# Attention with a local window, then a gated feed-forward: value products in 64-row tiles over two banks, merged ahead of the next scores in two of six units, and another plan

## The chip, the cores and the metric

The kernel runs on one core of a Trainium2 chip. The time of a kernel is the device time of one execution in microseconds; it is given as the median of the runs shown, with the lowest and highest. A profile is one further execution, recorded by the hardware profiler; it has a time of its own.

## The reference, cut to what matters

Each query sees the first 8 keys and the last 96 (its own included). A bias falls with the distance, with a slope for each head. The attention's output goes through two projections whose product is projected back.

```python
scores = scale * np.matmul(q, k.transpose(0, 1, 3, 2))
dist = np.where(is_global & ~is_local, float(n_local), np.abs(rel).astype(np.float32))
scores = np.where(keep, scores + bias, -1e9)          # bias = -slope[head] * dist
a = np.exp(scores - np.max(scores, axis=-1, keepdims=True))
a = a / (np.sum(a, axis=-1, keepdims=True) + 1e-09)
attn = np.matmul(a, v)                                # 4 x 8 heads x 768 x 64
x = attn.transpose(0, 2, 1, 3).reshape(B * S, H * D)  # 3072 x 512
out = (x @ w_a) * (x @ w_b) @ w_out                   # d_ff 1536
```

All inputs are float32 on the host but the weights, which arrive as 64-bit floating numbers and are turned into float32 on the chip.

## The kernel before, in words

**Units and granules.** The 3072 tokens are six units of 512 (`u` 0 to 5). The attention of a unit is four granules (`p` 0 to 3), each with 4 blocks of 128 queries for two heads. A granule's steps, in `granule_ops`: two score operations `r` of two blocks each, into one bank of PSUM for each head (`ps[h]`); the softmax on DVE and ACT (`t`, `sm`); a transpose of the probabilities; and the values. In unit 0 the transpose is done by PE (`direct`, tile `pt`), else by DVE into `tt` and then through DRAM: one DMA writes `mir`, eight DMAs read it back into `px` (the keys near the block: 104 rows) and `py` (the far keys: 64 rows for the first 64 queries of a block, 64 others for the last 64). All DMAs are issued by SP, in order.

**Scores (L581).** A block and head has 128 queries. TensorE is used in four quarters of 64 by 64: the row half is the head, the column half is the half `s` of the queries. For `s` = 1 one matmul is 168 columns wide, for `s` = 0 there are two, 104 and 64 wide. A float32 matmul shows as two instructions in the trace, each with a weight load.

**Values (L701).** For each block two pairs of matmuls add up in one bank `pa`: `px` with 104 rows and `py` with all 128 rows, each against one half `h` of 64 columns of weights and 128 columns wide. Half of `py` is zero: POOL writes the zeros once at the start (`zeros`, L535). `pa` is copied out in one piece, 128 x 512.

**Feed-forward.** `plain_product` (L943) for units 0 to 3 with the first three of six weight groups, `product` (L922) for the rest in a form with seven products instead of eight, `back` (L1099) for the last projection into the four banks `acc`. These use the whole array, 128 by 128.

**The order.** All operations are put on record with a due time and a cost for each engine that could do them. `Schedule.order` then replays the engines with these numbers: at each moment an engine takes the ready operation with the earliest due time whose banks and buffers are free. The result is the order of the instructions on every engine, and nothing is reordered later. The due times come from tables (`SPANS`, `CONV`, `QUADS0`, `HALF0` and others). In units 1, 2 and 3 (`LAGGED`) the values of granule `p` are recorded behind the scores of granule `p` + 1; in every unit they are due `VLAG` behind their scores. The scores take turns on the two banks `psS` and `psA`; `psA` serves the values too.

Of the kernel before, what the change touches and what calls it, by code (L numbers as in the profile page):

```python
# [57 lines left out]
SPANS = {1: (0.0, 0.6), 2: (0.85, 1.6), 3: (1.6, 2.6), 4: (3, 7), 5: (6.79, 11.5)}  # L58
NEAR = (0, 1, 2, 3)
CONV = {3: (1.72, 2.88), 4: (2.5, 3.5), 5: (4.39, 7), 2: (7.27, 10), 0: (10, 12.27), 1: (11.39, 14)}  # L60
# [11 lines left out]
LATER = {"psS": ("psS", "psA"), "psA": "psA", "psT": "psS"}  # L72
LAGGED = (1, 2, 3)
# [10 lines left out]
FORM0 = 2410.0  # L84
START = 25980.0
LOADLEAD = 7790.0
VLAG = 13280.0
PRICE = {"dve": 2.0}
BACKLOG = 1.0
TRACE = False  # L90
LAGS = {"pe": 200.0, "act": 270.0, "dve": 230.0, "pool": 290.0, "dma": 2300.0}
BIG = float(2**38)
HALF0 = 24080.0
HALF1 = 35730.0
STEPS0 = (-9.53, 6000.0, 17000.0, 25000.0)
QUADS0 = (4000.0, 3150.0, 9670.0, 13270.0, 22000.0, 25000.0)
QUADS1 = (28400.0, 31000.0, 36000.0, 35540.0, 46130.0, 44380.0)
QUADS2 = (48000.0, 51000.0, 54000.0, 51210.0, 58890.0, 63000.0)
GAP = 20220.0
# [34 lines left out]
class Op:  # L134
    def __init__(self, index, due, costs, emit, reads, writes, late, port):
        self.index, self.due, self.costs, self.emit, self.late = index, due, costs, emit, late
        self.port = port
        self.bufs, self.after, self.before = [], [], 0
# [18 lines left out]
class Schedule:  # L157
# [14 lines left out]
    def op(self, due, emit, reads=(), writes=(), late=0.0, port=(), **costs):  # L172

        self.ops.append(Op(len(self.ops), due, costs, emit, reads, writes, late, port))

    def order(self):
# [8 lines left out]
        port = 0.0  # L185

# [29 lines left out]
        while len(out) < len(self.ops):  # L216
            started = True
            while started:
                started = False
                for e in free:  # L220
# [8 lines left out]
                    else:  # L229
                        continue  # L230
                    for o in op.costs:
                        ready[o].remove(item)
# [8 lines left out]
                    free[e] = now + op.costs[e]  # L241
# [45 lines left out]
CN = 512  # L287


class Fast:  # L290
# [200 lines left out]
    def masks(self):  # L491
# [17 lines left out]
        op(-2e5, steps, [], [full], port=BOTH, dve=3 * dve(n, True) + 2 * dve(n))  # L509
        for hd in range(H):  # L510
# [3 lines left out]
                lambda e, p=p, h=h, hd=hd: nc.vector.tensor_scalar(  # L514
                    self.mask[p][:, h].rearrange("p a b -> p (a b)"),
                    rel(),
                    self.slope[:, hd : hd + 1],
                    None,
                    op0=ALU.mult,
# [4 lines left out]
                dve=dve(n, True),  # L524
            )

    def zeros(self):
        self.px = [self.sbuf([104, 4, 2 * NH, 32], F32, f"px{i}", f"px{i}") for i in range(PTBUFS)]
        self.py = [self.sbuf([P, 4, 2 * NH, 32], F32, f"py{i}", f"py{i}") for i in range(PTBUFS)]
        for py in self.py:  # L530
            for s in range(2):
                r = slice(64 * (1 - s), 64 * (1 - s) + 64)
                self.plan.op(
                    -1e6,
                    lambda e, py=py, r=r, s=s: self.nc.gpsimd.memset(py[r, 2 * s : 2 * s + 2], 0.0),  # L535
                    [],
                    [(py, "z%d" % s)],
                    pool=400,
                )
# [7 lines left out]
    def granule_ops(self, u, p, due, x, d, before):  # L547
        nc, op = self.nc, self.plan.op
        n = f"{u}_{p}"
        g = self.granule  # L550
        self.granule += 1
        px, py = self.px[g % PTBUFS], self.py[g % PTBUFS]
# [16 lines left out]
        for r in range(2):  # L569
# [4 lines left out]
            def scores(e, r=r, ps=ps):  # L574
                for b in range(2):
                    i = 2 * r + b
                    q0, k0, c0 = i * P, QN + i * KB, b * KW
                    for s, c, k, w in ((1, 0, 64, KW), (0, 0, 64, KX), (0, KX, 0, 64)):
                        for h in range(2):
                            rows = slice(64 * h, 64 * h + 64)  # L580
                            nc.tensor.matmul(  # L581
                                ps[h][64 * s : 64 * s + 64, c0 + c : c0 + c + w],
                                qk[rows, q0 + 64 * s : q0 + 64 * s + 64],
# [47 lines left out]
        if before:  # L631
            before()
# [176 lines left out]
    def attention(self, u, dues):  # L809
# [13 lines left out]
        if late:  # L823
            late()
# [777 lines left out]
```

## Time and profile before

| | |
|---|---|
| median of 3 runs | 725.11 us (724.22 to 725.52) |
| the profiled execution | 728.68 us |
| its span, first to last instruction | 726.4 us |
| PE busy | 693.5 us (95%), 5584 matmul instructions |
| DVE, ACT busy | 578.9 us (80%), 387.7 us (53%) |
| mean granted TensorE clock | 0.987 |

PE is TensorE's matmul side, PEld its weight loads, which overlap. Rows of the timeline give the start, the time that the merged instructions took up, the engine, the source line, the tiles and the count. Ends of matmuls are modelled, so the distance between starts is what the argument uses. The first 125 us hold the attention of units 0 and 1 and most of the conversions of weights that pass 0 needs; from there to 550 us the rest of the attention is worked in between the products; from 550 us on there is only feed-forward.

### The profile page before, as it was taken

What the parts mean: (1) busy time and instruction counts of PE and PEld (TensorE: products, weight loads), DVE (VectorE), ACT (ScalarE), POOL (GpSimd) and SP (SyncE); (2) the same over time, 40 slices, a digit from 0 to 9 for tenths busy, and PEclk for the clock granted to TensorE, in tenths of its full rate; (3) what the DMA queues carried; (4) which work ended last, traced back from release to release, by engine and by line L of the source; (5) the groups of instructions that cost most, each with busy time, mean ns of one, the idle gap of its engine ahead of it and who ended that gap; (6) DMA issues with size and microseconds to landing.
All of it is one profiled execution on the core that took longest, in us unless ns stands there. A gap on an engine that the chain in (4) does not pass through costs nothing.

```text
span 726.4 us, 15134 instructions
## 1 busy us (share of the span) xinstructions
PE 693.5 (95%) x5584; PEld 605.8 (83%) x5584; DVE 578.9 (80%) x1544; ACT 387.7 (53%) x989; POOL 1.8 (0%) x8
## 2 busy tenths in 40 slices
PE   5698998999999999999999999999999999999996
PEld 4487887777777788788899899899989999999995
DVE  7999997777687785799989898999999557746652
ACT  5987775745465673746455545666343434434310
POOL 1000000000000000000000000000000000000000
PEclk9799999999999999999999999999999999999999
DMA  8547998897989897776676888756794423343221
GB/s 296 213 163 259 269 294 300 267 305 250 304 280 303 253 335 247 262 266 228 221 249 232 294 259 301 245 201 230 233 337 151 146 59 102 131 145 102 74 73 62
DMA packets 67906, 162.39 MB, mean 224 GB/s; under 512 B 8432, under 2 KB 21872, under 8 KB 66032
## 3 DMA queue, kind: packets, MB, share of 16 engines
q1 hardware_dynamic: 67824, 161.34, 66.8%
q8 instruction: 46, 0.75, 0.4%
q14 instruction: 36, 0.29, 0.1%
HBM read 110.45 MB, written 50.86 MB: 222 GB/s over the span
## 4 chain that ended last, share of the span: by engine, by line
PE 68%; DMA 12%; DVE 11%; ACT 5%; issue 2%; SPq 1%; DVEq 0%; ACTq 0%
PE acc L1099 19%; PE al L922 16%; PE ga L922 12%; DMA wr<-wts 8%; PE ps L581 4%; PE pa L701 3%; ACT t L619 1%; DMA py<-mir 1%; DVE tt L677 1%; DMA X<-dx 1%; DVE t L602 1%; DVE wm L394 1%; ACT wm L369 1%; DVE wm L411 1%; SPq L323 1%
## 5 line engine op out<-in xcount | busy, mean ns | idle before, releaser
L1099 PE MATMUL acc<-w_O,hh 128*128 128x512 f32 x576 | 196.6, 400 | 0.0
L1099 PEld LDWEIGHTS acc<-w_O,hh 128*128 128x128 f32 x576 | 108.4, 188 | 25.1 <-issue 1.7
L1099 PE MATMUL acc<-w_O,hl 128*128 128x512 f32 x288 | 113.8, 395 | 0.4 <-DVE hl L342 0.3
L619 ACT ACTIVATE t<-t,sm 128x168 f32<-128x168 f32 x192 | 81.1, 424 | 20.2 <-DVE sm L602 20.0
L922 PE MATMUL al<-xf_T,w_S 128*128 128x256 f32 x576 | 76.8, 283 | 0.0
L922 PEld LDWEIGHTS al<-xf_T,w_S 128*128 128x128 f32 x576 | 72.2, 189 | 0.5
L332 ACT CAST hh<-h 128x512 fp32r<-128x512 f32 (+1 forms) x62 | 36.6, 592 | 50.2 <-DVE h L342 22.5
L1099 PEld LDWEIGHTS acc<-w_O,hl 128*128 128x128 f32 x288 | 54.3, 188 | 10.5 <-DVE hl L342 1.1
L581 PEld LDWEIGHTS ps<-qk 64*64 64x64 f32 x1152 | 36.3, 142 | 28.1 <-issue 14.2
L602 DVE CUSTOM_DVE_ANT_0 t<-ps,mask 128x168 f32<-128x168 f32 x192 | 53.3, 326 | 6.1 <-PE ps L581 5.6
L581 PE MATMUL ps<-qk 64*64 64x168 f32 (+2 forms) x1152 | 43.6, 278 | 14.4 <-DMA qk<-qk 7.0
L332 ACT COPY s<-al 128x512 f32<-128x512 f32 x47 | 27.5, 585 | 52.2 <-PE al L922 52.2
L369 ACT ACTIVATE wm<-wr 128x512 f32<-128x512 f32 x54 | 36.2, 670 | 34.7 <-DMA wr<-wts 25.2
L342 DVE TENSOR_TENSOR hl<-h,hh 128x512 fp32r<-128x512 f32 (+1 forms) x78 | 49.8, 642 | 5.2 <-ACT hh L332 4.9
L1031 DVE TENSOR_TENSOR s<-ga,s 128x512 f32<-128x512 f32 x48 | 32.8, 683 | 16.2 <-PE ga L922 16.0
L677 DVE STREAM_TRANSPOSE tt<-t 128x512 f32<-128x512 f32 x80 | 41.1, 552 | 0.8 <-ACT t L658 0.4
L404 ACT ACTIVATE wr<-wr 128x512 int32<-128x512 uint32 x54 | 36.2, 673 | 7.2 <-DMA wr<-wts 4.3
L701 PE MATMUL pa<-px,vt 104*64 104x128 f32 x384 | 38.9, 278 | 1.2 <-DMA px<-mir 1.2
L922 PE MATMUL ga<-xf_B,w_S 128*128 128x256 f32 x288 | 38.6, 283 | 1.3 <-ACT s L332 1.3
L922 PEld LDWEIGHTS al<-xf_B,w_A 128*128 128x128 f32 x288 | 37.5, 189 | 2.3 <-issue 0.3
L922 PE MATMUL ga<-xf_T,w_S 128*128 128x256 f32 x288 | 38.6, 283 | 0.6 <-DVE s L1031 0.5
L701 PE MATMUL pa<-py,vt 128*64 128x128 f32 x384 | 38.0, 273 | 1.1 <-DMA py<-mir 1.0
(274 smaller groups left out, 1318.6 us busy)
## 6 DMA issues: line engine op xcount, KB each, us to landing
wr<-wts SPq DMA_DIRECT2D x54, 512.0 KB
qk<-qk SPq DMA_DIRECT2D x24, 720.0 KB
mir<-tt SPq DMA_DIRECT2D x20, 768.0 KB
vt<-vd SPq DMA_DIRECT2D x24, 512.0 KB
X<-dx SPq DMA_DIRECT2D x10, 1024.0 KB
part<-o SPq DMA_DIRECT2D x32, 256.0 KB
wl_S<-dw_S SPq DMA_DIRECT2D x32, 256.0 KB
px<-mir SPq DMA_DIRECT2D x60, 128.0 KB
```

The source lines that it names most:

```text
L332: self.nc.scalar.copy(out(), src())
L342: lambda e: self.nc.vector.tensor_tensor(out(), a(), b(), op=op),
L369: lambda e: nc.scalar.activation(m(), high().bitcast(F32), AF.Abs),
L404: lambda e: nc.scalar.activation(low(), low().bitcast(U32), AF.Copy, scale=2.0**-29),
L581: nc.tensor.matmul(ps[h][64 * s : 64 * s + 64, c0 + c : c0 + c + w], qk[rows, q0 + 64 * s : q0 + 64 * s + 64], qk[rows, k0 + k : k0 + k + ...
L602: nc.vector.tensor_tensor_reduce(t[:, i, h], b[:, w], self.mask[pair][:, h, kind], -0.125, 3.0e38, ALU.add, ALU.min, sm[:, 0, j : j + 1],)
L619: lambda e, i=i, h=h, j=j: nc.scalar.activation(t[:, i, h], t[:, i, h], AF.Exp, bias=sm[:, 0, j : j + 1], scale=-1.0, accum_out=sm[:, 1, j ...
L677: nc.vector.transpose(dst[:, :, e0 : e0 + n], src[:, :, c0 : c0 + 32 * n].rearrange("p j (e k) -> p j e k", e=n),)
L701: nc.tensor.matmul(pa[64 * h : 64 * h + 64, i * P : i * P + P], vt[:lanes, v0 : v0 + 64], k[:, :, 2 * i + h], start=c == 0, stop=c == 1, s ...
L922: self.nc.tensor.matmul(bank[:, ab * HT : ab * HT + HT], w[:, a, (2 * ab + c) * P : (2 * ab + c) * P + P], x[:, b, c], start=first, stop=F ...
L1031: lambda e: nc.vector.tensor_tensor(s[:, :], bank[:, :], s[:, :], op=ALU.add),
L1099: self.nc.tensor.matmul(acc[i][:, :], a[:, rows], w[:, b], start=first and f == 0 and k == 0, stop=False, skip_group_check=True,)
```

## The change

**Values.** In units 1 to 5 `py` has only the rows and columns that are used (128 x 2 x 8 x 32), and no zeros. The values of a granule go into two banks, one for each half `s` of the queries. The `px` part is 104 rows by 64 columns of weights and 64 columns wide, for each `s` and `h`. The `py` part is a 64 by 64 quarter for each `s` and `h`, 64 columns wide. Unit 0 keeps the layout of before (`first`); its zeros stand in a tile `wide` that takes the place of `tt`.

**Merged.** In units 4 and 5 (`MERGED`) the values of granules 0, 1 and 2 have no operation of their own: half of their blocks is computed at the head of each score operation of the next granule, in columns 336 to 463 of the same two banks. They are copied out in four pieces. The values of the last granule, and those of units 1 to 3, stand alone (`alone`), in the banks `psS` and `psA`, and are copied out in two pieces.

**Scores.** Both halves `s` are now cut into 104 and 64 columns (`TILES`), in the order of the four quarters.

**Plan.** PE operations that use tiles have the mode "t"; when the next operation would change the mode, another ready one of the old mode may go first, if it is due within `KEEP`, and a change is charged `SWITCH`. `LEAN` and `LEAN1` shift the steps of a granule. Masks may be computed by ACT. The tables of due times have other numbers.

```diff
-SPANS = {1: (0.0, 0.6), 2: (0.85, 1.6), 3: (1.6, 2.6), 4: (3, 7), 5: (6.79, 11.5)}
+SPANS = {1: (0.0, 0.6), 2: (0.85, 1.3), 3: (1.96, 2.6), 4: (3, 7), 5: (6.83, 11.5)}
...
+MERGED = (4, 5)
...
-VLAG = 13280.0
+VLAG = 12680.0
...
+KEEP = 1500.0
+SWITCH = 250.0
...
+                    if e == "pe":
+                        if op.mode != mode:
+                            for other in ready[e]:
+                                if other[0] > op.due + KEEP:
+                                    break
+                                if other[2].mode == mode and fits(other[2]):
+                                    item, op = other, other[2]
+                                    break
...
+TILES = [(s, h, 0, 64, KX) for s in range(2) for h in range(2)]
+TILES += [(s, h, KX, (0, KW)[s], 64) for s in range(2) for h in range(2)]
...
+    def products(self, banks, c0, blocks):
+        nc, vt = self.fast.nc, self.vt
+        for c in range(2):
+            for b, i in enumerate(blocks):
+                for s in range(2):
+                    for h in range(2):
+                        v0 = (2 * i + c) * P + 64 * h
+                        rows = slice(64 * s, 64 * s + 64) if c else slice(0, 104)
+                        if c:
+                            moved = self.py[rows, :, 2 * i + h]
+                        else:
+                            moved = self.px[rows, 2 * s : 2 * s + 2, 2 * i + h]
+                        nc.tensor.matmul(
+                            banks[s][64 * h : 64 * h + 64, c0 + 64 * b : c0 + 64 * b + 64],
+                            vt[rows, v0 : v0 + 64],
+                            moved,
...
+                            tile_position=(64 * s if c else 0, 64 * h),
...
+    def take(self, due, banks, c0, r=None):
...
+            fast.copy(
+                due,
+                out,
+                lambda s=s: banks[s][:, c0 : c0 + 64 * n].rearrange("p (i c) -> p i c", c=64),
+                64 * n,
...
+    def alone(self):
...
+        tags = LATER["psS"]
+        banks = [fast.bank(tags[s], f"pv{self.u}_{self.p}_{s}") for s in range(2)]
...
             def scores(e, r=r, ps=ps):
+                if behind:
+                    behind.products(ps, 2 * KW, (2 * r, 2 * r + 1))
                 for b in range(2):
...
-                    for s, c, k, w in ((1, 0, 64, KW), (0, 0, 64, KX), (0, KX, 0, 64)):
-                        for h in range(2):
+                    for s, h, c, k, w in TILES:
...
+            if behind:
+                behind.take(due + lean[0], ps, 2 * KW, r)
```

What PE runs for the values of granule 1 of unit 2, which stand alone before and after. First in the order of before: `pa2_1` is the bank, `vt2_1` the values as weights.

```order
L701 MATMUL pa2_1_2129<-px0_248,vt2_1_1698 64x128 x2
L701 MATMUL pa2_1_2129<-py0_133,vt2_1_1698 64x128 x2
L701 MATMUL pa2_1_2129<-px0_248,vt2_1_1698 64x128 x2
L701 MATMUL pa2_1_2129<-py0_133,vt2_1_1698 64x128 x2
L701 MATMUL pa2_1_2129<-px0_248,vt2_1_1698 64x128 x2
L701 MATMUL pa2_1_2129<-py0_133,vt2_1_1698 64x128 x2
L701 MATMUL pa2_1_2129<-px0_248,vt2_1_1698 64x128 x2
L701 MATMUL pa2_1_2129<-py0_133,vt2_1_1698 64x128 x2
```

The same place in the order of the changed kernel, from the fifth pair of `px` on; `pv2_1_0` and `pv2_1_1` are the banks of the two halves of the queries.

```order
L334 MATMUL pv2_1_0_2310<-px0_261,vt2_1_1819 64x64 x2
L334 MATMUL pv2_1_1_2313<-px0_261,vt2_1_1819 64x64 x2
L334 MATMUL pv2_1_0_2310<-px0_261,vt2_1_1819 64x64 x2
L334 MATMUL pv2_1_1_2313<-px0_261,vt2_1_1819 64x64 x2
L334 MATMUL pv2_1_0_2310<-py0_1105,vt2_1_1819 64x64 x2
L334 MATMUL pv2_1_1_2313<-py0_1105,vt2_1_1819 64x64 x2
L334 MATMUL pv2_1_0_2310<-py0_1105,vt2_1_1819 64x64 x2
L334 MATMUL pv2_1_1_2313<-py0_1105,vt2_1_1819 64x64 x2
```

Sixteen matmuls of 128 columns have become 32 of 64 columns: first eight pairs with `px`, then eight pairs with `py`. The two kinds no longer alternate.

PE at granule 1 of unit 4, in the order of before: the first score operation of that granule, which follows a product `ga3_2_0` of the feed-forward. The values of granule 0 (`pa4_0`) stand ten operations earlier, in a place of their own.

```order
L581 MATMUL ps4_1_0_0_3646<-qk1_79 64x168
L581 MATMUL ps4_1_0_1_3648<-qk1_79 64x168
L581 MATMUL ps4_1_0_0_3646<-qk1_79 64x104
L581 MATMUL ps4_1_0_1_3648<-qk1_79 64x104
L581 MATMUL ps4_1_0_0_3646<-qk1_79 64x64
L581 MATMUL ps4_1_0_1_3648<-qk1_79 64x64
```

The same score operation in the changed kernel, from its head on.

```order
L334 MATMUL ps4_1_0_0_3998<-px0_261,vt4_0_3473 64x64 x2
L334 MATMUL ps4_1_0_1_4001<-px0_261,vt4_0_3473 64x64 x2
L334 MATMUL ps4_1_0_0_3998<-px0_261,vt4_0_3473 64x64 x2
L334 MATMUL ps4_1_0_1_4001<-px0_261,vt4_0_3473 64x64 x2
L334 MATMUL ps4_1_0_0_3998<-py0_1105,vt4_0_3473 64x64 x2
L334 MATMUL ps4_1_0_1_4001<-py0_1105,vt4_0_3473 64x64 x2
L334 MATMUL ps4_1_0_0_3998<-py0_1105,vt4_0_3473 64x64 x2
L334 MATMUL ps4_1_0_1_4001<-py0_1105,vt4_0_3473 64x64 x2
L717 MATMUL ps4_1_0_0_3998<-qk1_79 64x104
L717 MATMUL ps4_1_0_1_4001<-qk1_79 64x104
L717 MATMUL ps4_1_0_0_3998<-qk1_79 64x104
L717 MATMUL ps4_1_0_1_4001<-qk1_79 64x104
```

Two blocks of granule 0's values now stand in the same banks at the head of granule 1's scores, and the scores have four matmuls of 104 columns where there were two of 168 and two of 104.

More of the change, by code (lines that the diff above doesn't have):

```diff
@@ L230, in order @@
                         continue
+                    cost = op.costs[e]
+                    if e == "pe":
[6 more added lines that the diff above has]
+                                    break
+                        cost = op.costs[e] + (SWITCH if op.mode != mode else 0.0)
+                        mode = op.mode
                     for o in op.costs:
@@ L240, in order @@
                     out.append(op)
-                    free[e] = now + op.costs[e]
+                    free[e] = now + cost
                     if e in op.port:
@@ L631, in granule_ops @@
         if before:
-            before()
+            before.alone()
         tt = None
@@ L815, in attention @@
             self.xsaved[u] = d
-        late = None
+        behind = None
         for p in range(NPAIR):
-            then = self.granule_ops(u, p, dues[p], x, d, late)
-            if u in LAGGED:
-                late = then
-            else:
-                then()
-        if late:
-            late()
+            behind = self.granule_ops(
+                u, p, dues[p], x, d, behind if u in MERGED else None, behind if u in LAGGED else None
+            )
+            if p + 1 == NPAIR or u not in MERGED + LAGGED:
+                behind.alone()
+                behind = None
         return x
```

237 lines of the change are left out of this document (134 added, 103 removed).

## The prediction

> **What bounds the kernel now.** I read the page first, then the busy time by stage, then PE's own timeline, then its waits. The table by stage has, for each stretch, its length and the busy time of PE, PEld, DVE, ACT and POOL.
>
> ```profile
> core 0: us, PE busy (x) PEld busy (x) DVE busy (x) ACT busy (x) POOL busy (x), PEclk, DMA share, GB/s
> 0.00:20.00 20.00, 10.94 (x168) 9.42 (x168) 15.26 (x72) 11.08 (x37) 1.83 (x8) 1.00 0.78 273
> 20.00:60.00 40.00, 30.05 (x333) 25.08 (x327) 38.05 (x139) 35.66 (x118) 0.00 (x0) 0.86 0.59 210
> 60.00:125.00 65.00, 61.27 (x599) 54.01 (x600) 58.02 (x193) 44.34 (x127) 0.00 (x0) 0.97 0.86 274
> 125.00:300.00 175.00, 173.12 (x1304) 136.21 (x1303) 129.25 (x395) 100.83 (x282) 0.00 (x0) 0.99 0.86 285
> 300.00:550.00 250.00, 248.00 (x2041) 224.02 (x2040) 231.50 (x554) 137.96 (x329) 0.00 (x0) 1.00 0.75 250
> 550.00:720.00 170.00, 170.00 (x1154) 157.06 (x1152) 105.98 (x193) 57.87 (x102) 0.00 (x0) 1.00 0.32 102
> 720.00:726.40 6.40, 0.10 (x1) 0.00 (x0) 0.82 (x2) 0.00 (x0) 0.00 (x0) 0.87 0.41 148
> ```
>
> From 125 us to 720 us PE is idle for 1.9 + 2.0 + 0 us of 595: what shortens PE's work there shortens the run. From 20 to 60 us DVE is busy 38.05 of 40 and ACT 35.66, and PE is not the bound. From 300 to 550 us DVE has 18.5 us to spare, so a PE that is 2% faster does not make DVE the bound. The end (6.4 us) is the last eviction and its DMA. In the chain that ended last, pass 1 begins with this product:
>
> ```profile
> 124.05 4.55 PE al_0(0, 1)_1726 L943 x12
> ```
>
>
> A busy PE need not be at full rate, so I price PE's operations by distances between starts. Twelve matmuls of a product stand 1.43 us apart from the next twelve when nothing comes between (334.90 to 336.33). A score operation and a value operation between two products:
>
> ```profile
> 334.90 1.59 PE L922 MATMUL al<-xf_T,w_S 128*128 128x256 f32 x12
> 336.33 1.58 PE L922 MATMUL ga<-xf_B,w_S 128*128 128x256 f32 x12
> 337.84 0.82 PE L581 MATMUL ps<-qk 64*64 64x168 f32 x24
> 338.59 1.68 PE L922 MATMUL al<-xf_T,w_A 128*128 128x256 f32 x12
> 340.11 0.39 PE L1099 MATMUL acc<-w_O,hh 128*128 128x512 f32 x1
> ```
>
> From 336.33 to 340.11 is 3.78 us; two products are 2.86; the score operation costs 0.92 us.
>
> ```profile
> 400.74 1.59 PE L922 MATMUL al<-xf_T,w_S 128*128 128x256 f32 x12
> 402.26 0.44 PE L701 MATMUL pa<-px,vt 104*64 104x128 f32 x4
> 402.53 0.39 PE L701 MATMUL pa<-py,vt 128*64 128x128 f32 x4
> 402.75 0.39 PE L701 MATMUL pa<-px,vt 104*64 104x128 f32 x4
> 402.97 0.39 PE L701 MATMUL pa<-py,vt 128*64 128x128 f32 x4
> ...
> 403.85 0.39 PE L701 MATMUL pa<-py,vt 128*64 128x128 f32 x4
> 404.17 1.68 PE L922 MATMUL ga<-xf_T,w_S 128*128 128x256 f32 x12
> 405.69 1.59 PE L922 MATMUL al<-xf_T,w_S 128*128 128x256 f32 x12
> ```
>
> The value operation costs 4.95 - 2.86 = 2.09 us (400.74 to 405.69). Inside it four instructions take 0.22 us, in all eight groups: 1.76 us. The other 0.33 us lies at its two ends: going into the tiles and back to the whole array. Of the score's 0.92 us, 0.59 is then its own, for 2 x 2 x (104 + 64) = 672 columns that each quarter of the array streams: 0.88 ns a column. The values' 0.22 us are two steps of 128 columns, 0.86 ns a column, with the two halves side by side. Narrow steps run at the same rate:
>
> ```profile
> L581 PE MATMUL ps<-qk 64*64 64x168 f32 x384 | 42.2, 333 | 14.4 <-DMA qk<-qk 7.0 <-ACT X L332 2.6 <-DVE sm L602 1.9
> L581 PE MATMUL ps<-qk 64*64 64x104 f32 x384 | 35.4, 275 | 0.0
> L581 PE MATMUL ps<-qk 64*64 64x64 f32 x384 | 28.4, 227 | 0.0
> ```
>
> If a step of 64 columns took as long as one of 104, a quarter with 8 such steps would need 8 x 0.091 = 0.73 us, and the operation 1.06, not 0.92. So I take 0.056 us for a step of 64 columns.
>
> **The change part by part.** *Values alone* (units 1 to 3, and the last granules of 4 and 5: 14 granules). The `px` part has 16 steps of 64 columns instead of 8 of 128: the same time. The `py` part has 8 steps of 64 with four quarters side by side, instead of 8 of 128: that is what the zeros cost before, 0.44 us. New is a change from 128-row to 64-row tiles inside. No row shows that change alone with both sides busy; it is bounded by nothing and by a whole entry and exit, 0.33. I take half, 0.17, since one border is crossed. Sum: 0.33 + 0.17 + 24 x 0.056 = 1.84 us, so 0.25 saved; 14 x 0.25 = 3.5 us. The Trainium skill, TensorEngine Tiling (Array Packing), Key Properties, says that a change of the tiling mode drains TensorE; that agrees with the 0.33 us at the ends of these operations, and it speaks against this part, but it gives no price.
>
> *Values merged* (6 granules). Each half is 0.33 + 0.17 + 12 x 0.056 + 0.59 = 1.76 us, a granule 3.52. Before it was 2 x 0.92 + 2.09 = 3.93. Saved: 0.41, six times 2.5 us. The 26 inner changes of both parts are the largest unknown: at nothing the two parts save 10.4 us, at 0.33 each they save 1.8.
>
> *Equal score tiles.* A quarter streamed 168 columns or 104 + 64 before and streams 104 + 64 now: no gain. The two matmuls more per block run beside the others.
>
> *The plan.* In the orders of PE I count the stretches of tile operations between whole-array ones: 63 before, 61 now. Merging takes six away, so the new plan has four more elsewhere, all in units 0 and 1. Four at 0.33 are 1.3 us, and about half lies where PE is the bound: +0.7 us.
>
> *Start.* Three of eight mask operations go to ACT, two of them ahead of the first softmax.
>
> ```profile
> 8.44 1.31 DVE L514 TENSOR_SCALAR mask<-X,slope 128x336 f32<-128x336 f32 x4
> 9.66 0.33 DVE L602 CUSTOM_DVE_ANT_0 t<-ps,mask 128x168 f32<-128x168 f32 x1
> ...
> 9.91 0.33 DVE L602 CUSTOM_DVE_ANT_0 t<-ps,mask 128x168 f32<-128x168 f32 x1
> ```
>
> DVE starts the softmax two masks earlier, 0.65 us, if the scores are there; ACT does its masks while it waits for it. ACT, which the chain runs over next, has three operations more, so I take -0.4. The rest of the first 60 us is a new order of the same work on two full engines; I take 0, with 3 us either way.
>
> *Waits.* PE runs in order, so an operation that waits for `px` holds all products behind it.
>
> ```profile
> PE ga L922 <- ACT s L332: 1.3, 2, 0.9
> PE pa L701 <- DMA px<-mir: 1.2, 1, 1.2
> PE pa L701 <- DMA py<-mir: 1.0, 3, 0.4
> ```
>
> Before, the values waited 2.2 us in all, most of it in unit 2:
>
> ```profile
> 177.58 0.44 PE L701 MATMUL pa<-px,vt 104*64 104x128 f32 x4 [1.16 <-DMA px<-mir]
> 178.39 0.44 PE L701 MATMUL pa<-py,vt 128*64 128x128 f32 x4 [0.37 <-DMA py<-mir]
> ```
>
> In the new order the PE work between a granule's scores and its values is shorter by 0 to 3 us in units 1 to 3, while the way through DVE and the DMAs is as long: I add 0.7 us. Against that `py`, which lands last, is needed half an operation later. In three merged places only two `back` operations stand between the two score operations, which use the same banks; four softmax steps 0.25 us apart (9.66 to 9.91) and two copies must be through by then: +0.5 us. Most other places have one or two products (1.43 each) there, and the same wait is hidden. The copies out are one to three instructions more a granule; ACT's idle time hides them (112 us of 250 from 300 to 550 us), and were it gone DVE would take them within its 18.5.
>
> *Sum.* -3.5 - 2.5 + 0.7 - 0.4 + 0.7 + 0.5 = -4.5 us. The profiled execution took 728.68 us (span 726.4 and 2.3 around it); it would be 724.2. It lies 3.6 above the median of 725.11; the forecast for the median is 720.6 us.
>
> **The rivals.** *A narrow step has a floor (slower).* If 64 columns cannot be streamed faster than the weights change, each of the 24 steps costs more than 0.056. The place is the `px` part, where both halves use the same rows. At s us a step the two parts change by 20 x (24 s + 0.17 - 1.76) - 6 x 0.33; with the other terms (+1.5) that is zero at s = 0.0675. At 0.091, a step of 104 columns, the parts change by +9.9 and all by +11.4: 736.5 us. For it speaks that a weight load is long:
>
> ```profile
> L701 PEld LDWEIGHTS pa<-px,vt x384: 132/136/139, 16.9 to 517.8; 104*64 104x64 f32 x192
> ```
>
> Against it: 0.136 us of load is longer than the step of 0.11 us that the values make now, so loads are hidden already, and the score's quarters step through 64 columns without loss. The Trainium skill, TensorE: Matmul & The Clock Gate, Part 3, says that a weight load overlaps a running matmul only where the row groups differ; by that rule the `px` part would pay each load; at the page's figure for a load (1 ns for 1.2 columns, 53 ns for 64) that is, as an estimate, 20 x 16 x 0.053 = 17 us more, 737.6. The steps of 0.11 us, all with the same row groups, disagree with it. Chance 0.07.
>
> *The new plan's waits take the gain (no change).* One wait like that of unit 2's third granule (1.2 us for `px`, 0.4 for `py`) in half of the twelve granules of units 1 to 3 is 9.6 us, less the 2.2 there now: +7.4 instead of the 0.7 taken, 727.3 us. With three such waits it is 722.5. I take the middle, 724.9. For it: the shorter distances. Against it: the planner puts values where it takes `px` as landed, and its numbers for DMAs are unchanged. Chance 0.17.
>
> *The first 125 us get shorter (faster still).* PE is idle there for 9.1 + 10.0 + 3.7 us. Seven are the first load; of the other 16 a better order could take 5: 715.5 us. For it: all tables for this part have new numbers. Against it: the same operations stand there, and both DVE and ACT are full from 20 to 60 us. Chance 0.16.
>
> *The inner change is dear.* At 0.33 us each the sum is -0.3: 724.8 us, no change. Chance 0.06.
>
> **How the numbers follow.** The forecast has 0.54: 720.6 us, by its own range 717 to 723.5. About 0.2% (1.45 us) is what a measurement can tell from no change. Faster by more: 0.50 of the forecast's, 0.16, 0.06 of the waits and 0.03 of the dear change's, 0.75. Within: 0.04 + 0.08 + 0.03 = 0.15. Slower: 0.07 for the floor and 0.03 for waits, 0.10. The range, 8 in 10, leaves out the floor and the far ends: 714.0 to 725.0.
>
> **What would show it.** In the profile of the changed kernel a value operation alone between two products should cost 1.84 us, its `px` groups stepping at 0.056, and a merged operation 1.76; scores alone still 0.92. PE's idle time from 125 us on should stay near 4 us, with the waits for `px` at 2 to 4 us in all. The prediction is wrong if the steps are above 0.0675 us, if the inner change is near 0.33, or if the feed-forward of pass 1 starts over 3 us earlier or later than at 124 us.

## The result, and the profile after

The changed kernel takes 733.62 us (median of 8 runs, 730.66 to 740.97), the kernel before 725.93 in the same comparison: a ratio of 1.013, with a 95% interval of 1.009 to 1.017. It is 7 to 12 us slower, where 4.5 us faster was forecast. One execution of the kernel before took 2328.69 us; it counts in that median of 8, but not in the ratio. The profiled execution took 740.97 us (span 739.1), 7.4 above its median, so its waits are on the long side: the two profiled executions are 12.3 us apart, the medians 7.7. Busy times by stage, with the columns of before:

```profile
60.00:125.00 65.00, 60.37 (x803) 53.04 (x795) 54.54 (x185) 43.37 (x126) 0.00 (x0) 0.97 0.85 264
125.00:200.00 75.00, 70.56 (x772) 54.84 (x771) 57.71 (x192) 44.14 (x139) 0.00 (x0) 1.00 0.89 301
200.00:300.00 100.00, 94.63 (x844) 74.62 (x843) 71.59 (x203) 54.57 (x151) 0.00 (x0) 0.98 0.78 266
300.00:425.00 125.00, 122.59 (x1190) 109.25 (x1188) 109.54 (x269) 69.15 (x167) 0.00 (x0) 1.00 0.74 248
425.00:550.00 125.00, 121.94 (x1222) 110.58 (x1222) 116.42 (x285) 67.55 (x174) 0.00 (x0) 1.00 0.76 249
550.00:715.00 165.00, 165.00 (x1141) 153.55 (x1140) 107.59 (x196) 60.48 (x108) 0.00 (x0) 1.00 0.35 114
```

From 125 to 550 us PE is idle for 4.4 + 5.4 + 2.4 + 3.1 = 15.3 us; before it was 3.9. PE's own steps did become shorter. PE's timeline around values that stand alone, and around merged ones:

```profile
407.38 1.58 PE L1006 MATMUL ga<-xf_B,w_A 128*128 128x256 f32 x12
408.90 1.15 PE L334 MATMUL pv<-px,vt 104*64 104x64 f32 x32
409.98 0.69 PE L334 MATMUL pv<-py,vt 64*64 64x64 f32 x32
410.60 1.70 PE L1006 MATMUL al<-xf_T,w_S 128*128 128x256 f32 x12
412.14 1.59 PE L1006 MATMUL ga<-xf_T,w_S 128*128 128x256 f32 x12
...
447.04 0.69 PE L334 MATMUL ps<-px,vt 104*64 104x64 f32 x16
447.65 0.46 PE L334 MATMUL ps<-py,vt 64*64 64x64 f32 x16
447.94 0.77 PE L717 MATMUL ps<-qk 64*64 64x104 f32 x32
448.63 1.68 PE L1006 MATMUL ga<-xf_T,w_S 128*128 128x256 f32 x12
450.15 1.58 PE L1006 MATMUL al<-xf_T,w_S 128*128 128x256 f32 x12
451.67 0.69 PE L334 MATMUL ps<-px,vt 104*64 104x64 f32 x16
```

From 407.38 to 412.14 are 4.76 us; less two products (2.86) the values alone cost 1.90, against 2.09 before. From 447.04 to 451.67 are 4.63; less 2.86, a merged half costs 1.77. The `px` part alone has 16 steps and takes 1.08 us up to the `py` part (408.90 to 409.98); in a merged half it has 8 and takes 0.61 (447.04 to 447.65). So eight steps cost 0.47 us, a step 0.059, and what is left, 0.14, is the change of tiles inside. By these rows PE's work fell by 14 x 0.19 + 6 x (3.93 - 3.54) = 5.0 us. It came to nothing, because PE waits. PE's waits over the whole run, without two rows of its start:

```profile
...
PE ps L717 <- DVE sm L741: 3.8, 4, 2.5
PE ps L717 <- ACT X L462: 3.8, 3, 2.6
PE pv L334 <- DMA px<-mir: 3.5, 5, 1.1
...
PE ga L1006 <- ACT s L462: 1.9, 2, 1.0
```

The longest of these, 2.6 us for ACT X, is in the chain of waits at the start of unit 4 (start, length, what; the chain is read downwards, each piece releasing the next):

```profile
258.14 5.49 DMA wr<-wts
263.63 0.02 issue
263.65 0.04 ACTq L534
263.69 0.04 issue
263.74 0.59 ACT wr L534
264.32 0.33 ACT X L462
264.66 0.04 issue
264.70 0.81 PE ps L717 x23
265.51 0.94 PE acc L1183 x3
266.45 4.31 PE al_0(0, 1)_3637 L1027 x12
...
274.50 2.78 PE al_1(0, 1)_3722 L1027 x12
```

A load of raw weights is 5.49 us under way. ACT, which works in order, stands at the conversion that needs it (L534). Behind that, in ACT's queue, is the copy of the second half of the values out of a score bank (L462), and the next score operation needs that bank. So a weight DMA that has nothing to do with the attention stops PE for 2.6 us. The clock falls as well: the 12 matmuls of a product behind the stop take 4.31 us, 8 us later 2.78 (the granted clock is 0.83 from 260 to 270 us, 1.00 in the ten before and after). The Trainium skill, TensorE: Matmul & The Clock Gate, Part 1, gives the rule, that PE which idles through a window of about 3.4 us loses its full clock; here the slow product stands behind a wait of only 2.6 us. It is no part of the loss behind 124 us: in before the clock falls once there in the same way (0.88 from 125 to 135 us), behind a wait of 1.7 us, and the product that begins pass 1 takes 4.62 us there, against 3.04 in the changed kernel.

ACT waits more for these loads than it did. The row of the first conversion step, after:

```profile
L499 ACT ACTIVATE wm<-wr 128x512 f32<-128x512 f32 x54 | 36.1, 671 | 48.3 <-DMA wr<-wts 37.7
```

And the same row of before:

```profile
L369 ACT ACTIVATE wm<-wr 128x512 f32<-128x512 f32 x54 | 36.2, 670 | 34.7 <-DMA wr<-wts 25.2
```

The first theory, then (B): two banks for values alone hold the next scores until ACT, blocked by weight loads, has copied both pieces. Rivals: the new plan's due times alone bring the waits (P); merging does (M).

### The profile page after: what moved, and what is told of

The parts are those of the page before. It is cut to its first block, busy times and chain, and to the rows that moved or that the text cites. A ratio compares the mean times of both kernels' runs of the same rounds, so it can differ in the third digit from the quotient of the medians.

```text
span 739.1 us, 17229 instructions
## 1 busy us (share of the span) xinstructions
PE 694.5 (94%) x6608; PEld 606.0 (82%) x6608; DVE 577.8 (78%) x1543; ACT 391.3 (53%) x1022; POOL 1.8 (0%) x8
## 4 chain that ended last, share of the span: by engine, by line
PE 33%; DVE 26%; DMA 25%; ACT 9%; issue 4%; SPq 2%; DVEq 0%; ACTq 0%
PE acc L1183 12%; PE al L1006 10%; PE ga L1006 8%; DMA wr<-wts 7%; DMA mir<-tt 5%; DVE tt L816 3%; DVE t L741 3%; ACT t L758 3%; DMA px<-mir 2%; SPq L453 2%; DVE t L800 2%; DMA X<-dx 2%; DVE hl L472 2%; DMA wl_S<-dw_S 1%; DMA part<-o 1%
## 5 line engine op out<-in xcount | busy, mean ns | idle before, releaser
L462 ACT CAST hh<-h 128x512 fp32r<-128x512 f32 (+1 forms) x65 | 38.2, 589 | 47.8 <-DVE h L472 18.7
L499 ACT ACTIVATE wm<-wr 128x512 f32<-128x512 f32 x54 | 36.1, 671 | 48.3 <-DMA wr<-wts 37.7
L717 PEld LDWEIGHTS ps<-qk 64*64 64x64 f32 x1536 | 38.0, 142 | 28.7 <-issue 11.4
L717 PE MATMUL ps<-qk 64*64 64x104 f32 (+1 forms) x1536 | 45.1, 250 | 16.8 <-DMA qk<-qk 7.5
L462 ACT COPY s<-al 128x512 f32<-128x512 f32 x47 | 27.5, 585 | 57.9 <-PE al L1006 57.8
L506 DVE TENSOR_SCALAR wm<-wm 128x512 f32<-128x512 f32 x54 | 22.6, 420 | 35.1 <-ACT wm L499 35.1
L534 ACT ACTIVATE wr<-wr 128x512 int32<-128x512 uint32 x54 | 36.3, 673 | 17.3 <-DMA wr<-wts 17.1
L1006 PE MATMUL ga<-xf_B,w_A 128*128 128x256 f32 x288 | 38.5, 283 | 1.1 <-DVE h L1072 1.1
```

Of the source, the lines that this page charges most:

```text
L462: self.nc.scalar.copy(out(), src())
L499: lambda e: nc.scalar.activation(m(), high().bitcast(F32), AF.Abs),
L506: lambda e: nc.vector.tensor_scalar(m(), m(), EMIN, EMAX, op0=ALU.max, op1=ALU.min),
L534: lambda e: nc.scalar.activation(low(), low().bitcast(U32), AF.Copy, scale=2.0**-29),
L717: nc.tensor.matmul(ps[h][64 * s : 64 * s + 64, c0 + c : c0 + c + w], qk[rows, q0 + 64 * s : q0 + 64 * s + 64], qk[rows, k0 + k : k0 + k + ...
L1006: self.nc.tensor.matmul(bank[:, ab * HT : ab * HT + HT], w[:, a, (2 * ab + c) * P : (2 * ab + c) * P + P], x[:, b, c], start=first, stop=F ...
```

## The experiments

Each run is compared with the kernel before on the same chip; microseconds in brackets are the ratio's 95% interval times the time of before.

### Tiles or plan

**New tiles, old plan.** All tables as before; grouping by mode, shifts and masks on ACT off:

```diff
-CONV = {3: (1.72, 2.88), 4: (2.92, 3.5), 5: (4.14, 7), 2: (7.27, 9.59), 0: (10, 12.27), 1: (11.39, 14)}
+CONV = {3: (1.72, 2.88), 4: (2.5, 3.5), 5: (4.39, 7), 2: (7.27, 10), 0: (10, 12.27), 1: (11.39, 14)}
...
-LEAN1 = (-900.0, 0.0, 0.0, 0.0, 480.0, 0.0)
+LEAN1 = (0.0, 0.0, 0.0, 0.0, 0.0, 0.0)
```

> The changed kernel's value tiles, merging and score tiles, with every number of the plan as before (due times, no grouping by mode, no shifts of steps, masks on DVE alone). Theory B (the banks): the values stand alone on both score banks now, so the next scores wait until ACT has copied out both pieces, and ACT stands behind weight conversions that wait for a DMA; that needs no new plan, so most of the loss stays: 729 to 734 us, with PE waits on ACT X of 2 us or more. Theory P (the new plan's due times alone bring the waits): the PE work saved (about 5 us) shows, 719 to 722 us. Theory M (merging in units 4 and 5): as B here, 729 to 734, but with the waits after 300 us.

Measured: 1.0115 (1.0072 to 1.0159), +8.4 us. As theory B says in size, but not in place: its longest PE wait behind the first load is 4.6 us at 96 us, for DVE's softmax, and waits for ACT X are 0.8 in all.

**Old tiles, new plan.** The kernel before with all of the plan's numbers and rules:

```diff
-VLAG = 13280.0
+VLAG = 12680.0
...
+KEEP = 1500.0
+SWITCH = 250.0
```

> The kernel before with its tiles, one bank for the values and no merging, but the whole new plan (due times, grouping by mode, shifts, masks on ACT). Theory B: without the second bank the scores do not wait for copies: 723 to 728 us, no change from before. Theory P: the waits come with the plan: 730 to 736 us, with ACT idle for the weights' DMA at 30 us or more, as in the changed kernel (37.7 against 25.2 before). Theory M: 723 to 728 us.

Measured: 1.0244 (1.0204 to 1.0285), +17.8 us, more than any of the three expected. Theory B has no place for that: the plan by itself costs more than the whole change. But P fails too, by the run above. Tiles and plan do not add up: each alone is about as slow as both, or slower.

**Not merged.**

```diff
-MERGED = (4, 5)
+MERGED = ()
```

> The changed kernel with MERGED empty: the values of units 4 and 5 stand alone in the new tiles, right behind their granule as before. Costs at least 6 x 0.2 us of PE. Theories B and P: the loss lies between 190 and 280 us, in units 3 and the start of 4, which stays: 732 to 737 us. Theory M: the loss after 300 us goes, 727 to 731 us.

Measured: 1.0168 (1.0126 to 1.0211), +12.2 us, slower than any of the three expected. Merging does not bring the loss. M is out.

**Weights loaded earlier.**

```diff
-            due - 6000.0,
+            due - 9000.0,
...
-        raw = self.sbuf([P, 2 * CN], I32, "wraw", "wr" + n, 2)
+        raw = self.sbuf([P, 2 * CN], I32, "wraw", "wr" + n, 3)
```

> The changed kernel with the load of each group of raw weights due 9 instead of 6 us ahead of its conversion, and three buffers for raw weights instead of two. Theory B in the form that the late weight DMA holds ACT, and ACT the copies: ACT idle for wr falls from 37.7 us to under 20, PE's waits on ACT X from 3.8 us to under 1, and the time falls by 3 to 6 us, to 727 to 731. If the late DMA is not what holds PE: 732 to 736 us, whatever ACT's idle time does.

Measured: 1.0119 (1.0084 to 1.0154), as slow as the change. ACT's wait for these loads in L499 fell to 22.5 us, and PE's for ACT X only to 2.9; the plan came out with another order and other waits. The total does not decide; where the time went is told below.

### The order alone

The four runs share one thing: the planner made another order. So the next ones hold the order, or change nothing else.

**New tiles in the order of before.** The tiles, nothing merged; the planner gets the durations of before, and both pieces of a copy are one step:

```diff
-            self.due, lambda e: self.products(banks, 0, range(NH)), self.reads, banks, pe=1300
+            self.due, lambda e: self.products(banks, 0, range(NH)), self.reads, banks, pe=1900
...
-        for s in range(2):
-            fast.copy(
+        fast.plan.op(
+            due,
+            both,
```

> The new value tiles and score tiles, no merging, at the order of before: the planner is given the durations and numbers of before, and both pieces of a value copy go as one step, so SP's order is that of before row for row, and DVE's and ACT's but for the copies. Theory T (the tiles give what their steps say, the order took it away): 16 granules in units 2 to 5 save 0.1 to 0.25 us each, unit 1 some: 2 to 4 us faster than before. Theory B (two banks hold up the next scores): 2 us or more slower than before, PE waits on ACT X or on px longer by as much.

Measured: 1.0042 (1.0011 to 1.0073), +3.0 us (0.8 to 5.3). Even here the tiles gain nothing. In the profile about 1.9 us of it lie behind the last product (8.6 us against 6.7; see the last section); ahead of that no loss can be told from zero.

**The same, merged** (the edit is against the run above).

```diff
-MERGED = ()
+MERGED = (4, 5)
```

> As the run with the tiles at the order of before, but units 4 and 5 merged; until unit 4 the order is nearly that of before. Theory T: merging saves 0.41 us for each of 6 granules more: 4.5 to 6.5 us faster than before. If the two score operations of a merged granule stand too close, so that the second waits for softmax and copies: no faster than the unmerged run, with PE waits on DVE sm or ACT X after 300 us of 2 us or more.

Measured: 1.0073 (1.0041 to 1.0105), +5.3 us. No gain from merging, though a merged half between two products costs PE 1.78 us here.

**Only the planner's durations.** The kernel before, told other costs:

```diff
-            op(due, scores, [qk], ps, pe=720)
+            op(due, scores, [qk], ps, pe=620)
...
-        op(due + VLAG, values, [vt] + pr, [pa], pe=1900)
+        op(due + VLAG, values, [vt] + pr, [pa], pe=1300 if u else 1760)
```

> The kernel before, instruction for instruction the same work; only the planner is told that scores take 620 instead of 720 ns and values 1300 instead of 1900, so it makes another order. If the order of before is better than what the planner makes of slightly other numbers (theory T's other half): 3 to 10 us slower than before. If any such order is as good: within 2 us.

Measured: 1.0189 (1.0148 to 1.0230), +13.7 us (10.7 to 16.7), for the same work in another order. This alone is as much as the change lost, or more. Two rows of its PE waits over the run:

```profile
PE ps L581 <- DVE sm L602: 6.6, 6, 2.6
PE pa L701 <- DMA px<-mir: 3.8, 2, 3.5
```

Before they were 1.9 and 1.2 us.

**The late plan of before.** The changed kernel with four numbers back:

```diff
-SPANS = {1: (0.0, 0.6), 2: (0.85, 1.3), 3: (1.96, 2.6), 4: (3, 7), 5: (6.83, 11.5)}
+SPANS = {1: (0.0, 0.6), 2: (0.85, 1.6), 3: (1.6, 2.6), 4: (3, 7), 5: (6.79, 11.5)}
...
-LOADLEAD = 8130.0
+LOADLEAD = 7790.0
```

> The changed kernel with four of its numbers as before: the due times of units 1 to 5 and of the later conversions of weights (SPANS, CONV), VLAG and LOADLEAD. The start (unit 0, its shifts, pass 0's weights, masks) stays new. If the due times of units 2 to 4 and of the conversions make the waits between 190 and 280 us: they go, PE is idle there for under 3 us instead of 9.8, and the time is 721 to 727 us. If it is the start's numbers or the tiles: 732 to 738 us.

Measured: 1.0159 (1.0109 to 1.0209), +11.5 us. PE's idle time from 200 to 300 us fell from 5.4 to 2.9, and others grew. These four numbers do not make the loss.

**Where the loss stands.** The first product of pass 1 divides every run: the feed-forward ahead of it is the same in all. From each run's one profile, in microseconds:

| run | first product of pass 1 starts at | from there to the start of the last matmul | from there to the end |
|---|---|---|---|
| before | 123.98 | 595.7 | 6.7 |
| copy in two pieces (below), order of before | 125.10 | 593.3 | 6.6 |
| the changed kernel | 123.98 | 607.3 | 7.8 |
| old tiles, new plan | 121.47 | 610.2 | 7.8 |
| new tiles, old plan | 134.05 | 589.2 | 7.5 |
| weights loaded earlier | 133.56 | 590.4 | 8.2 |
| only the planner's durations | 130.68 | 597.8 | 6.6 |
| new tiles in the order of before | 125.85 | 594.2 | 8.6 |

With all of the work of before and in its order, that first product started anywhere from 120.97 (the run with less DVE work, whose edit starts later) to 125.10 us, so differences of a few us are noise. The large ones say that the loss has two places. With the new tables it stands behind that product. With the old tables and new durations, and with the weights loaded earlier, it stands ahead of it, in the first 134 us. Behind it, the new tiles with the old plan have 4.0 us of waits and take 4.1 and 6.5 us less than the first two rows. About 0.7 of that is a score operation that lies ahead instead, and 1.6 of the larger one is the slow clock in before. So a shorter PE may have shown there, as far as one execution each can tell. And loading the weights earlier cut PE's waits behind that product from 15.3 to 5.4 us, in line with theory B, and lost as much ahead of it. Those for ACT X fell only from 3.8 to 2.4, and the order was another as well, so B is not shown as the whole cause.

### What a shorter PE is worth

The prediction rests on one sentence: what shortens PE's work there shortens the run. These runs test it in the kernel before, with every engine in its order. `c` = 1 is the `py` part: in units 1 to 5 the first kernel leaves the far keys out, the second adds them twice.

```diff
-                for c in range(2):
+                for c in range(1 if u else 2):
```

> The kernel before, every engine in its order, but the values of units 1 to 5 leave out the far keys (the products with py): 4 groups of 0.22 us less in each of 20 granules, 17.6 us of PE work, 14.1 of it in units 2 to 5. Theory F (PE alone sets the time from 125 us on, as the prediction took it): 13 to 17 us faster than before. Theory G (work that PE saves at this order comes up against loads and DVE steps that come no earlier, so that it is given back): 3 to 9 us faster, with new PE waits on DVE after 300 us.

Measured: 0.9944 (0.9916 to 0.9971), -4.1 us (-6.1 to -2.1) for 17.6 us of PE work, 3.5 of it in unit 1.

```diff
-                for c in range(2):
+                for c in (0, 1, 1) if u else (0, 1):
```

> The kernel before, every engine in its order, but the products with py in units 1 to 5 are made twice: 17.6 us more of PE work. Theory F: 14 to 18 us slower. Theory G says the same or a little less here, 12 to 18, since PE has only about 4 us of idle time from 125 us on to take it up: the time rises by nearly all that PE gets more and falls by only part of what it gets less.

Measured: 1.0203 (1.0165 to 1.0240), +14.7 us (12.0 to 17.4). What PE gets more costs 84%; what it gets less brings 23%. Where the saving is lost:

```diff
-                for c in range(2):
+                for c in range(1 if u in (4, 5) else 2):
```

> As the run with less value work, but the far keys are left out in units 4 and 5 alone: 8 granules x 0.88 = 7.0 us of PE work, all between 300 and 550 us, every engine in the order of before. Theory G, in the form that DVE (busy 231.5 of 250 us there) and what feeds it set that stretch: within 2 us of before. Theory F: 6 to 7 us faster.

Measured: 0.9995 (0.9968 to 1.0023): no change that can be seen (-2.3 to +1.7 us), for 7.0 us. And with `u in (1, 2, 3)`:

> The far keys left out in units 1 to 3 alone: 12 granules x 0.88 = 10.6 us of PE work before 300 us. Theory G: this is where PE's time counts (DVE is busy 129 of 175 us from 125 to 300), so it carries the gain of the run with less value work in all units, 4 us, or more if DVE does not take it back later: 3 to 9 us faster, the lead shrinking after 300 us. Theory F: 9 to 10.6 us.

Measured: 0.9952 (0.9932 to 0.9972), -3.5 us (-4.9 to -2.0), a third of 10.6. So the gain comes from units 1 to 3, all of it as far as can be seen, and from 300 to 550 us a shorter PE is worth a third of what it saves at most. In the run with less work in units 4 and 5:

```profile
125.00:300.00 175.00, 175.00 (x1325) 137.78 (x1326) 134.60 (x415) 106.03 (x298) 0.00 (x0) 1.00 0.88 291
300.00:550.00 250.00, 245.91 (x1930) 221.04 (x1929) 232.14 (x549) 135.67 (x319) 0.00 (x0) 1.00 0.75 250
```

PE is busy 248.0 of 250 us there in before, and 245.9 here: part of the saving may stand as idle time. One profile cannot show it: from 125 to 300 us, where nothing was changed, the two differ by 1.9 us as well. This execution was also 2.2 us below its median and that of before 3.6 above. Is it DVE's own work that holds PE? The next two runs leave out one DVE step of each weight conversion that is due late, 23 steps of 0.68 us, 16 of them between 300 and 550 us in before; the first also leaves the far keys out.

```diff
-            lambda e: nc.vector.scalar_tensor_tensor(
+            lambda e: due > 290000.0 or nc.vector.scalar_tensor_tensor(
```

> As the run with less value work in all units, and DVE besides leaves out one step (the one that joins sign and exponent, 0.68 us) of each conversion of weights due after 290 us: 16 of them, 10.9 us, between 300 and 550 us. Theory G (DVE's own work sets that stretch): the 7 us of units 4 and 5 come out too, 8 to 14 us faster than before, against 4 without. If it is loads and not DVE's work: 3 to 6 us, as without.

> The kernel before, values whole, with the same DVE steps left out: the control. If PE's own work is what the stretch has left when DVE is lighter (idle 2.0 us of 250): 0 to 2.5 us faster. If DVE alone set it: 4 us or more faster.

Measured: 0.9927 (0.9900 to 0.9953), -5.3 us, with both; 0.9968 (0.9948 to 0.9987), -2.3 us, with DVE's steps alone. Together they bring about what they bring apart (-4.1 and -2.3): the 7 us of units 4 and 5 do not come out. DVE's own work is worth something, but it is not what holds them back.

What can hold PE is seen at one place. In the run with the new tiles in the order of before, all engines:

```profile
329.73 0.32 SPq L456 DMA_DIRECT2D wl_O<-dw_O  x1
...
332.20 0.43 DVE L467 CAST w_O<-wl_O 128x512 fp32r<-128x512 f32 x1 [2.51 <-DMA wl_O<-dw_O]
332.55 0.68 DVE L1117 TENSOR_TENSOR s<-ga,s 128x512 f32<-128x512 f32 x1
...
333.29 0.99 PE L1008 MATMUL ga<-xf_T,w_S 128*128 128x256 f32 x6 [2.07 <-DVE s L1117]
```

The same place in before:

```profile
330.96 0.32 SPq L323 DMA_DIRECT2D wl_O<-dw_O  x1
...
332.29 0.43 DVE L334 CAST w_O<-wl_O 128x512 fp32r<-128x512 f32 x1 [1.36 <-DMA wl_O<-dw_O]
...
333.37 0.86 PE L922 MATMUL ga<-xf_T,w_S 128*128 128x256 f32 x5 [0.50 <-DVE s L1031]
```

The faster PE comes 1.6 us earlier to this point and goes on at the same time, 333.29 against 333.37. The weights land at the same time although their load was issued 1.2 us earlier. DVE stands at them, and the small step that PE needs (0.68 us) stands behind that on DVE.

### Loads and copies

So I brought loads forward on SP, in the run with the tiles and, as the control, in before:

```diff
-            for o in order:
+            for o in forward(order):
```

> The new tiles at the order of before (as in that run), and on SP the loads of weights and activations for coming passes (wl, X<-dx) go up to six DMAs earlier where nothing they depend on is passed; PE, DVE and ACT keep their order. Theory G: the wait of DVE for wl_O at 330 us, which held PE 2.1 us, and those for X<-dx at 500 and 524 us shrink, and the run is 1.5 to 4 us faster than with the tiles alone: 0.2% slower to 0.3% faster than before. If these loads are not what gives the gain back: as with the tiles alone, 0.3 to 0.6% slower than before.

> The kernel before with the same loads brought forward on SP and nothing else, the control. Theory G: in before PE waits only 4 us in all from 125 us on, so little is to be had: within 1.5 us of before. If it is as much faster as the run with the new tiles is against the tiles alone, the loads are a gain of their own and say nothing of the tiles.

Measured: 1.0120 (1.0078 to 1.0163) and 1.0069 (1.0043 to 1.0095): both slower, by 8.7 and 5.0 us. DVE's waits for loads from 125 to 600 us in the control:

```profile
DVE o L1166 <- DMA o<-part: 7.0, 3, 3.4
```

In before no wait of DVE for `o<-part` is listed there. What goes forward puts other loads back. The Trainium skill, DMA: Bandwidth & Descriptors, Issuing engines are not separate DMA queues, says that all DMAs run on the same 16 engines and interleave; these waits are in line with it. The expectation that the gain would return fell.

What the tiles cost where the order is held was tried in two parts. The copy in two pieces alone, in before:

```diff
-        self.copy(due + VLAG, lambda: vt[:, :T], lambda: pa[:, :], T, [pa], [vt], psum=True)
+        self.taken(due + VLAG, lambda: vt[:, :T], (lambda: pa[:, :],) * 2, ([pa], [vt]))
```

> The kernel before with old tiles and one bank for the values, every engine in its order; only the copy of the values out of the bank in units 1 to 5 is made in two pieces of 256 columns, as the new tiles need (0.36 us each instead of 0.62 us in one). If the second piece is what costs at the same order (ACT holds the next scores 0.1 us longer in 20 places, and what stands behind it): 1.5 to 4 us slower than before. If not: within 1 us.

Measured: 0.9996 (0.9975 to 1.0016). The pieces cost nothing that can be seen (-1.8 to +1.2 us). And the new value tiles in units 1 to 3 alone:

```diff
+        if u in (1, 2, 3):
+            tags = LATER["psS"]
+            banks = [self.bank(tags[s], f"pv{u}_{p}_{s}") for s in range(2)]
```

> The new value tiles in units 1, 2 and 3 alone, with the zeros, the scores, unit 0 and units 4 and 5 as before, every engine in the order of before. 12 granules save 0.2 us of PE work each. Theory G: the saving counts in part before 300 us and nothing new is paid after it: 0.5 to 2.4 us faster than before. If the tiles cost by themselves wherever they stand (the copies, the banks): 0.5 to 3 us slower.

Measured: 1.0042 (1.0012 to 1.0072), +3.1 us. The loss is as large as with the tiles in all units. About 1.6 us of it lie behind the last product (8.2 against 6.6, last section). The rest is inside the interval, and not settled: in its profile PE's waits for ACT X from 62 to 130 us are 3.5 us against 1.6 with the copy in two pieces, and one of them is new:

```profile
83.36 0.66 ACT L369 ACTIVATE wm<-wr 128x512 f32<-128x512 f32 x1 [2.22 <-DMA wr<-wts]
83.92 0.66 ACT L404 ACTIVATE wr<-wr 128x512 int32<-128x512 uint32 x1
84.48 0.63 ACT L773 COPY X<-pv 128x256 f32<-128x256 f32 x2
84.89 0.91 PE L581 MATMUL ps<-qk 64*64 64x168 f32 x15 [1.30 <-ACT X L773]
```

In before the same conversion ran at 81.23 without a wait, the copy at 82.40, and the scores at 83.78 did not wait. It is again a weight load, 2.1 us later in this execution, with the copy behind it on ACT. Why it is later with these tiles is not shown. No version tried is faster than before with all its work done.

## Why the prediction was wrong

Two steps failed: the worth of PE's time (its saving of 6.0 us) and, by more, the waits of a new order (its +0.7 and +1.2).

- **"What shortens PE's work there shortens the run"**: this step failed. PE's idle time of 1.9 + 2.0 us was read as a proof that PE alone sets the time. It shows only that in this order PE is hardly ever seen waiting. The loads and steps around it stood nearly as tight: at the order of before a shorter PE brings 23%, in units 4 and 5 nothing that can be seen, a longer one costs 84%. By that 23% the 6.0 us of the two parts were worth about 1.4 us, as an estimate, before any new wait. Besides, 4 of the 14 granules priced there, those of unit 1, lie ahead of 125 us, outside the stretch that the sentence speaks of.
- **The plan, +0.7 us** (four more stretches of tile operations): this failed by more. The wrong thing was counted. A new order is not the sum of its mode changes. The same work in an order made from slightly other durations costs +13.7 us, moving some loads on SP alone +5.0, the new plan with the old tiles +17.8.
- **Waits +0.7 for `px`, +0.5 for merged places**: mis-sized and misplaced. From 125 to 550 us PE's idle time rose by 11.4 us in the profiled executions. Of its listed waits there (14.9 us up to 560, before 3.7) `px` is 2.0; copies behind ACT are 3.8, softmax steps 3.3, and most of the rest inputs of the feed-forward that ACT or DVE brought late.
- **"ACT's idle time hides" the copies out**: wrong in kind. ACT's idle time is not room. Over the run 37.7 us of it are waits, in order, for weight loads at one conversion step, and what is queued behind them, the copies, waits too. The row was there to be read in before: 25.2 us, and a score operation that waited 1.7 us for ACT X.
- **Values alone 1.84 us, step 0.056, inner change 0.17**: nearly right. Measured 1.90, 0.059 and 0.14; saved 0.19 a granule instead of 0.25.
- **Merged half 1.76**: right, 1.77. It saved PE time in the stretch where that is worth little or nothing.
- **Equal score tiles, 0**: right; a score operation between two products takes 0.93 us before and in the run with the tiles in the order of before.
- **Start -0.4, rest of the first 60 us 0 +/- 3**: it came out, in part by luck. The product that begins pass 1 starts at 123.98 us in both traces, but other new orders began it up to 10 us later.
- **The end**, which has no term in the sum: 7.8 us from the last matmul on, against 6.7.
- **Rivals**: no floor of narrow steps. Its formula gives the merged granules one inner change where the working has two; with two, zero lies at 0.065 us a step and not 0.0675. The new plan's waits were the right rival, at a far too low price: half of twelve granules with 1.6 us for `px` and `py`. It was priced by the wait that the trace already showed, not by what a new order can bring.

By the runs, the way from 4.5 us faster to 9.4 slower is about: tiles in the order of before +3.0, merged +5.3, in an order made from their true durations +8.4, with the new tables +9.4. That each of these is slower than before is clear of the noise; each has an interval of 2 to 3 us either way, so the distances between them are not.

## What to carry to other kernels

A PE that is busy 99% of the time under a fitted order is not the only bound: leave some of its work out, and put some in twice, at the same order, before pricing a shorter PE; if less work brings little and more costs nearly all, loads and other engines stand nearly as tight as PE. A shorter operation also changes what the planner makes of everything else. In such a kernel a change of planner inputs is to be priced by a control that changes the order alone (here 1.9%), not by the work moved. Split each profile at an operation that all versions share before looking for one cause: here the same size of loss stood in the first 134 us of some runs and behind them in others. And idle time of an in-order engine that waits for DMAs is a block in front of whatever is queued behind it.

## What else the runs showed of the chip

Between the start of the last matmul and the end of the span lie 6.7 us in before and 6.6 with the copy in two pieces, but 8.2 with the new tiles in units 1 to 3 and 7.8 in the changed kernel. In the run with the new tiles in units 1 to 3, SP waits at the very end on its own queue:

```profile
SPq L1494 <- SPq L1494: 1.8, 1, 1.8
```

Over the 20 profiles that stretch is 6.0 to 7.0 us in the 11 programs with up to 841 recorded instructions on SP, and 7.5 to 8.6 in the 9 with 843 or more. In each of the nine there is a gap of 1.3 to 1.9 us right behind the 841st instruction, wherever that stands among the last ones. The new tiles at the order of before make 844 of 841, so about 1.6 us of their loss has nothing to do with PE. What happens in the gap is open. In the changed kernel it lasts from 737.25 to 738.78 us and a packet of the queue `instruction` starts at 737.21; but before has such a packet near its end too (725.63), and no gap.

Steps of 64 columns with a weight load each run at 0.059 us, in the `px` part with the same 104 rows in each of them, and the inner change from 104-row to 64-row tiles costs 0.14.
